# Moving w_in's shifted words and the values of single tiles to PSUM banks of their own, in a banded-attention and two-layer FFN kernel

## The chip, the cores and the metric

One core of a Trainium2 chip (trn2) runs the kernel. The metric is the device time of one execution in microseconds (us). A measured time is the median of several executions. The profiled execution is a further one, with the hardware profiler on.

## What is computed

Causal attention with a window of 64 positions over 8 batches, 8 heads, 576 positions and head dimension 64, in float32. Its output, as 4608 tokens of 512 features, goes through a two-layer network whose middle function is the identity for positive values and a factor alpha per feature for negative ones.

```python
scores = (1 / sqrt(D)) * q @ k.transpose(0, 1, 3, 2)
mask = (rel >= 0) & (rel < 64)
scores = where(mask, scores, -1e9)
attn = exp(scores - max(scores))
attn = attn / (sum(attn) + 1e-9)
x = (attn @ v).transpose(0, 2, 1, 3).reshape(4608, 512)
h = x @ w_in
g = maximum(h, 0) + alpha * minimum(h, 0)
out = g @ w_out
```

The weights w_in (512 x 2048) and w_out (2048 x 512) are passed to the kernel as 64-bit words and made into floats on the chip.

## The kernel before

**Tiles and blocks.** The 4608 tokens are 36 tiles of 128, and 4 tiles are a block, so there are 9 blocks of 512 tokens. For each tile the kernel computes scores (`score`, L448, on TensorE, into a pair of score banks `S_BANK[t % 2]`, banks 2 and 3 or 4 and 5), the masked row minimum of the negated scores for each of 8 heads (`take_least`, L457, VectorE), the exponentials and their sums (`exponential`, L464, ScalarE, 8 per tile), the reciprocal of the sums (`invert`, L468 and L469, VectorE), the scaled weights (`scale`, L473, GpSimd, called POOL in the profile), their transposes, the value matmuls (`value`, L504, TensorE) and x, split into a high part xh (L576 on ScalarE or L577 on VectorE) and a low part xl (L578, VectorE). The values lie in banks 6 and 7 (`V_BANK`).

**Single tiles.** The first eight tiles are attended one by one (`attend_one`), with due times from the list `SINGLE`. They are transposed on TensorE (`turn`, L488) back into their own score banks, and copied out of them (`take_turned`, L492). The values of a single tile lie in the first half (columns 0 to 255) of each of banks 6 and 7. Later tiles go in pairs (`attend_two`), whose values fill both halves; most of those are transposed on VectorE (L481, L483).

**First layer.** A cell is one block times one chunk of 128 of the 2048 middle features, in 12 matmuls of 128 x 512 (`cell`, L646: four of xh with the weight's high part wh, four of xl with wh, four of xh with the low part wl). The result in a bank (`H_BANK`, 0 or 1 in turn) is evicted by ScalarE (L652, the slope) and VectorE (L653, the maximum), and stored to memory by a DMA of SP's queue. A cell needs x of all four tiles of its block. For block 0, the first three chunks (`EARLY_HALVES`) are done as half cells of two tiles each, so that they can start when tiles 0 and 1 have x. Two half cells in a row share a bank and a buffer, one in each half. Due times come from `HALVES`, `PACE` and, for later blocks, `BEGIN` and `CELL`.

**Conversion of w_in.** Meanwhile `convert_in` makes the 16 chunks of w_in from 64-bit words (`chunk`). SP loads a chunk into one of three raw buffers (L343). ScalarE converts the low words (L352, ulps). VectorE scales the high words into PSUM (L357, "rebias"), shifts them there (L368) and joins them with the sign (L370) into `val`; POOL adds the ulps (L372). ScalarE or POOL makes wh (L325) and POOL or VectorE wl (L322). The shifted words, `aside`, lie in the second half (columns 256 to 511) of banks 6 and 7, in one two-bank tile `twin`; every chunk uses the same place.

**Second layer.** After all first-layer cells, `second` multiplies with w_out in a form with seven products in place of eight (L750).

**The order.** Every step is an `Op` with engine, assumed duration, keys that it reads and writes, and a due time (`add`). `Program.order` plays these on a model of the five engines, and gives each engine its instructions in the order of due time among those that are ready in the model. Then they are emitted in that order, and the framework inserts the semaphore waits that the tiles' accesses call for. The keys are what the planner knows of conflicts: `bank.6.0` and `bank.6.1` are two halves of bank 6, which it takes as independent. A step marked `paired` is modelled as sharing a port with POOL. From the end of `ident` until the half cell `h.0.1.0` is placed, the planner fills TensorE's gaps with matmuls of the identity (`warm`, L307). The four small operations `signs` (L312 to L315, VectorE) derive the slope from alpha.

Of the kernel before, what the change touches and what calls it, by code (L numbers as in the profile page):

```python
# [9 lines left out]
F32 = mybir.dt.float32  # L10
# [183 lines left out]
def banded_attention_then_prelu_ffn(  # L194
# [67 lines left out]
    staged = [stage[:, i] for i in range(2)]  # L262
    raws.append(stage.rearrange("p x t -> p (x t)").bitcast(I32))

    banks = [psum.tile([P, 512], F32, name=f"bank_{i}") for i in range(6)]
    twin = psum.tile([P, 1024], F32, name="bank_6")
    banks += [twin[:, :512], twin[:, 512:]]
    aside = twin.rearrange("p (x t) -> p x t", x=2)[:, :, 256:]
    H_BANK, S_BANK, V_BANK = (0, 1), ((2, 3), (4, 5)), (6, 7)

    hidden = [[far.tile([P, 4, 2, HW], F32, name=f"g_{n}_{d}") for d in range(DUOS)] for n in range(NB)]
# [7 lines left out]
    def add(name, engine, busy, emit, *args, **kw):  # L279
        p.add(name, {engine: (busy, emit)}, *args, **kw)  # L280
# [33 lines left out]
        nc.vector.tensor_tensor(out=slope, in0=sign, in1=alpha_p, op=ALU.mult)  # L314
        nc.vector.tensor_scalar(out=flip, in0=sign.bitcast(I32), scalar1=-2**31, scalar2=None, op0=ALU.bitwise_and)  # L315

    add("signs", "DVE", 0.5, signs, ["alpha"], ["signs"])


    def subtract_of(out, a, b):  # L320
# [14 lines left out]
    def chunk(name, c, f, second, start=0.0):  # L335
        r = raw_at[0] % (2 if second else RAWS)
        ulps, k_ulps = ulp_ring[raw_at[0] % 2], f"e.ulps.{raw_at[0] % 2}"
        raw_at[0] += 1
        raw = raws[r]
        if second:  # L340
            load = lambda: nc.sync.dma_start(raw, w_out[f * P:(f + 1) * P, :])
        else:
            load = lambda: nc.sync.dma_start(raw.rearrange("p (c f) -> p c f", c=NP),  # L343
                                             w_in[:, 2 * f * P:2 * (f + 1) * P].rearrange("(c p) f -> p c f", p=P))
        pairs = raw.rearrange("p (n t) -> p n t", t=2)
        low, high = pairs[:, :, 0].bitcast(U32), pairs[:, :, 1]
        at = val[:, c]
        bits = at.bitcast(I32)
        k_raw, k_val = ["e.staged.0", "e.staged.1"] if r == 2 else [f"e.raw.{r}"], f"e.val.{c}"
        both = keys(k_val + "a", k_val + "b")  # L350
        add("raw." + name, "SP", 0.5, load, (), keys(*k_raw), service=1.7, earliest=start)
        add("rd." + name, "ACT", 0.57, lambda: nc.scalar.activation(ulps, low, AF.Copy, scale=2.0**-29), k_raw, keys(k_ulps), earliest=start)  # L352
        two_of = lambda v: v.rearrange("p (x t) -> p x t", x=2)
        k_aside = [f"bank.{b}.1" for b in V_BANK]
        by_vector = not second and f in REBIASED
        if by_vector:
            add("rb." + name, "DVE", 0.64, lambda: nc.vector.tensor_scalar(  # L357
                out=aside, in0=two_of(high).bitcast(F32), scalar1=2.0**-112, scalar2=None, op0=ALU.mult), k_raw, k_aside, earliest=start)
        else:
            add("rb." + name, "ACT", 0.57, lambda: nc.scalar.activation(at, high.bitcast(F32), AF.Copy, scale=2.0**-112), k_raw, [*keys(k_val), *both], earliest=start)  # L360
        if second:
            add("sh." + name, "DVE", 0.52, lambda: nc.vector.tensor_scalar(
                out=bits, in0=bits, scalar1=3, scalar2=flip[:, f:f + 1], op0=ALU.logical_shift_left, op1=ALU.bitwise_or), ["signs"], [k_val], earliest=start, paired=True)
            add("sg." + name, "DVE", 0.62, lambda: nc.vector.scalar_tensor_tensor(  # L364
                out=bits, in0=high, scalar=-2**31, in1=bits, op0=ALU.bitwise_and, op1=ALU.bitwise_xor), k_raw, [k_val], earliest=start, paired=True)
        else:
            from_ = aside.bitcast(I32) if by_vector else two_of(bits)
            add("sh." + name, "DVE", 0.62, lambda: nc.vector.tensor_scalar(  # L368
                out=aside.bitcast(I32), in0=from_, scalar1=3, scalar2=None, op0=ALU.logical_shift_left), [] if by_vector else [k_val], k_aside, earliest=start)
            add("sg." + name, "DVE", 0.64, lambda: nc.vector.scalar_tensor_tensor(  # L370
                out=two_of(bits), in0=two_of(high), scalar=-2**31, in1=aside.bitcast(I32), op0=ALU.bitwise_and, op1=ALU.bitwise_xor), [*k_raw, *k_aside], [*keys(k_val), *both], earliest=start)
# [120 lines left out]
        copy(turned[t % 2][:, u].rearrange("p h u b q -> p b h u q"),  # L492
             banks[from_[u]].rearrange("p (b h u q) -> p b h u q", b=2, h=2, u=2))

    def value(t, i):
        av = [bank_of(b).rearrange("p (i a) q -> p i a q", i=2)[:, i] for b in V_BANK]
        pt, at = turned[t % 2].rearrange("p a h u b q -> p a h (u b q)"), 2 * (t % KRING)
        for a in range(2):
            for block, to, from_ in ((1, slice(0, P), slice(W, 3 * W)), (0, slice(0, W), slice(0, W)),
                                     (2, slice(W, P), slice(3 * W, 4 * W))):  # L500
                for h in range(2):
                    for x in range(2):
                        r, hs = slice(x * W, (x + 1) * W), slice(h * D, (h + 1) * D)
                        nc.tensor.matmul(av[x][hs, a, to], vring[r, a, at + block, hs], pt[r, a, h, from_],  # L504
                                         start=block == 1, stop=block == 2)
# [56 lines left out]
    def x_keys(part, slot, tiles=range(BT)):  # L562
        return [f"{part}.{slot}.{i}" for i in tiles]

    def x_parts(ts):
        n, i = divmod(ts[0], BT)
        here = slice(i * P, (i + len(ts)) * P)
        if len(ts) == 1:
            pieces = [(range(2), [part.rearrange("p (a x) t -> p x a t", x=2)[:, :, :, here] for part in xs[n % 2]],
                       twin.rearrange("p (x i a q) -> p x i a q", x=2, i=2, a=2)[:, :, 0], [f"bank.{b}.0" for b in V_BANK])]  # L570
        else:
            pieces = [([x], [part.rearrange("p (a x) (i q) -> p x i a q", x=2, q=P)[:, x, i:i + 2] for part in xs[n % 2]],
                       bank_of(V_BANK[x]).rearrange("p (i a) q -> p i a q", i=2), halves_of(V_BANK[x])) for x in range(2)]
# [7 lines left out]
    def attend_one(t, begin, pace):  # L581
# [4 lines left out]
                [key for a in pairs for key in (f"e.q.{t % 2}.{a}", *ring_keys("k", t, [a]))], [f"bank.{b}.{a}" for b in S_BANK[t % 2] for a in pairs], key=begin)  # L586
        softmax(t, True)
        turned_by_pe(t, S_BANK[t % 2], begin + 0.5 * pace)
        add(f"av.{t}", "PE", 1.0, lambda: value(t, 0), [*ring_keys("v", t), *pt_keys(t)], [f"bank.{b}.0" for b in V_BANK], key=begin + pace)
        x_parts([t])  # L590

    def values_of(ts, key):
        def emit():
# [34 lines left out]

    def cell(n, f, key, m=None):

        at = counted[0] + (counted[0] % 2 if m is None else 0)
        counted[0] = at + (2 if m is None else 1)
        bank, c = H_BANK[at // 2 % 2], at // 2 % len(cells)
        d, j, x = f % 8 // 2, f % 2, f // 8
        parts = [0, 1] if m is None else [at % 2]
        half = slice(0, 2 * HW) if m is None else slice(m * HW, (m + 1) * HW)
        to = slice(parts[0] * HW, (parts[-1] + 1) * HW)
        h, g = banks[bank][:, to], cells[c][:, to]
        k_h, k_g = [f"bank.{bank}.{i}" for i in parts], [f"cell.{c}.{i}" for i in parts]
# [222 lines left out]
```

## Time and profile before

| | |
|---|---|
| median of 3 runs | 851.5 us (850.8 to 851.97) |
| profiled execution | 852.4 us, span 850.6 us |
| busy: TensorE, VectorE, ScalarE, POOL | 838.3, 694.0, 438.3, 201.3 us |
| HBM read, written | 95.95 MB, 55.57 MB |

The profile's page gives busy times by engine; a line number there is that of the kernel file. "Idle before" a group of instructions names what the engine waited for last. PE is TensorE's matmul stream, DVE VectorE, ACT ScalarE. A busy time of PE is modelled, and matmuls overlap each other slightly.

### The profile page before, as it was taken

To read this page: it belongs to the slowest core of one execution; us is meant where nothing else is said; L and a number is where in the kernel's file an instruction comes from. 1 tells how busy PE (TensorE), PEld (TensorE's weight loads), DVE (VectorE), ACT (ScalarE), POOL (GpSimd) and SP (SyncE) were. 2 spreads that over 40 slices of the span, in tenths; PEclk is the share of its full clock that TensorE was granted. 3 is DMA by queue.
4 is the path that set the end of the run, shared out by engine and by line. 5 is a ranking of instruction groups with operands and counts; after the bars stand their busy time and mean duration, and the time that the engine had idled before them with its cause. 6 is when DMAs were issued, how large, how long until landed. Compare 5 with 4: busy or idle time off the path is not lost.

```text
span 850.6 us, 21098 instructions
## 1 busy us (share of the span) xinstructions
PE 838.3 (99%) x7850; PEld 758.5 (89%) x7850; DVE 694.0 (82%) x1777; ACT 438.3 (52%) x1111; POOL 201.3 (24%) x189
## 2 busy tenths in 40 slices
PE   8899999999999999999999999999999999999998
PEld 8778888888888888888888889999999999999998
DVE  5778898998989979898894647979798888879883
ACT  5777755556655565556643434444444444444441
POOL 5777414355611065212640000000000000000000
PEclk9999999999999999999999999999999999999999
DMA  8778655555655567656555997545354444545201
GB/s 253 232 238 253 212 164 195 161 163 201 212 162 174 185 227 247 200 177 220 190 203 183 319 307 256 164 111 169 110 156 137 139 135 137 150 126 164 84 27 50
DMA packets 121287, 152.91 MB, mean 180 GB/s; under 512 B 10592, under 2 KB 92512, under 8 KB 121184
## 3 DMA queue, kind: packets, MB, share of 16 engines
q1 hardware_dynamic: 120896, 151.30, 56.0%
q8 instruction: 62, 1.02, 0.5%
q14 instruction: 41, 0.34, 0.1%
q10 hardware_dynamic: 288, 0.26, 0.1%
HBM read 95.95 MB, written 55.57 MB: 178 GB/s over the span
## 4 chain that ended last, share of the span: by engine, by line
PE 90%; DVE 5%; DMA 2%; ACT 2%; issue 1%; SPq 0%; POOL 0%; DVEq 0%; POOLq 0%; ACTq 0%
PE bank L750 41%; PE bank L646 40%; PE bank L504 4%; PE bank L448 4%; DVE pt L481 1%; PE bank L488 1%; DVE cell L653 1%; ACT w L464 1%; DMA g<-g 1%; PE bank L307 1%; DMA v<-vN 1%; DVE pt L483 1%; DVE w L457 0%; DMA g<-cell 0%; DVE bank L368 0%
## 5 line engine op out<-in xcount | busy, mean ns | idle before, releaser
L722 ACT CAST yh<-g 128x512 fp32r<-128x512 f32 x216 | 133.0, 622 | 142.1 <-PE bank L750 85.9
L652 ACT ACTIVATE cell<-bank,alphas 128x512 f32<-128x512 f32 (+1 forms) x147 | 99.6, 678 | 160.1 <-PE bank L646 154.7
L723 DVE TENSOR_TENSOR yl<-g,yh 128x512 fp32r<-128x512 f32 x216 | 147.6, 687 | 26.1 <-ACT yh L722 25.0
L646 PE MATMUL bank<-xh,wh 128*128 128x512 f32 (+1 forms) x588 | 158.7, 392 | 0.5 <-DVE cell L653 0.2
L750 PE MATMUL bank<-wh,yh 128*128 128x256 f32 x1008 | 155.9, 277 | 0.0
L750 PE MATMUL bank<-wh,yl 128*128 128x256 f32 x1008 | 155.8, 277 | 0.0
L750 PE MATMUL bank<-wl,yh 128*128 128x256 f32 x1008 | 155.8, 277 | 0.0
L646 PE MATMUL bank<-xl,wh 128*128 128x512 f32 (+1 forms) x588 | 155.0, 385 | 0.0
L646 PE MATMUL bank<-xh,wl 128*128 128x512 f32 (+1 forms) x588 | 154.7, 385 | 0.0
L653 DVE SCALAR_TENSOR_TENSOR cell<-bank,alphas,cell 128x512 f32<-128x512 f32 (+1 forms) x147 | 108.0, 737 | 47.2 <-ACT cell L652 41.3
L750 PEld LDWEIGHTS bank<-wh,yh 128*128 128x128 f32 x1008 | 133.5, 188 | 0.2
L750 PEld LDWEIGHTS bank<-wh,yl 128*128 128x128 f32 x1008 | 133.5, 188 | 0.0
L750 PEld LDWEIGHTS bank<-wl,yh 128*128 128x128 f32 x1008 | 133.4, 188 | 0.0
L646 PEld LDWEIGHTS bank<-xl,wh 128*128 128x128 f32 x588 | 109.2, 188 | 22.6
L646 PEld LDWEIGHTS bank<-xh,wh 128*128 128x128 f32 x588 | 106.6, 188 | 25.2 <-DVE cell L653 2.9
L646 PEld LDWEIGHTS bank<-xh,wl 128*128 128x128 f32 x588 | 109.2, 188 | 22.2
L464 ACT ACTIVATE w<-w,nm 128x128 f32<-128x128 f32 x288 | 111.6, 390 | 25.0 <-DVE nm L457 25.0
L473 POOL TENSOR_TENSOR w<-w,rc 128x512 f32<-128x512 f32 x72 | 74.3, 1052 | 117.0 <-DVE rc L469 90.5
L481 DVE STREAM_TRANSPOSE pt<-w 32x256 f32<-32x256 f32 x192 | 83.7, 436 | 10.0 <-POOL w L473 6.7
L717 DVE TENSOR_TENSOR g<-g,g 128x512 f32<-128x512 f32 x108 | 74.2, 687 | 1.8
L457 DVE CUSTOM_DVE_ANT_0 w<-bank,masks 128x128 f32<-128x128 f32 x288 | 63.0, 285 | 7.4 <-PE bank L448 7.2
L372 POOL TENSOR_TENSOR val<-val,ulps 128x512 int32<-128x512 int32 x32 | 41.5, 1301 | 102.6 <-DVE val L364 91.2
(62 smaller groups left out, 717.7 us busy)
## 6 DMA issues: line engine op xcount, KB each, us to landing
g<-g SPq DMA_DIRECT2D x144, 256.0 KB, 3.4
g<-cell SPq DMA_DIRECT2D x141, 256.0 KB, 3.0
out<-cell SPq DMA_DIRECT2D x36, 256.0 KB, 2.5
q<-qT SPq DMA_DIRECT2D x35, 256.0 KB, 5.2
raw<-w_out SPq DMA_DIRECT2D x16, 512.0 KB, 5.1
v<-vN SPq DMA_DIRECT2D x18, 384.0 KB, 5.3
k<-kT SPq DMA_DIRECT2D x17, 384.0 KB, 4.6
raw<-w_in SPq DMA_DIRECT2D x11, 512.0 KB, 4.4
```

Of the source, the lines that this page charges most:

```text
L372: add("jn." + name, "POOL", 1.27, lambda: nc.gpsimd.tensor_tensor(out=bits, in0=bits, in1=ulps, op=ALU.add), [k_ulps], [k_val, *both], ear ...
L457: nc.vector.tensor_tensor_reduce(out=of_head(weights[t % 2], g), in0=bank_of(S_BANK[t % 2][x])[:, e].rearrange("p (b k) -> p b k", b=2), i ...
L464: nc.scalar.activation(w, w, AF.Exp, scale=-1.0, bias=least[t % 2][:, g:g + 1], accum_out=sums[:, t % 2, g, 0:1])
L473: nc.gpsimd.tensor_tensor(out=w, in0=w, in1=rc.unsqueeze(1).unsqueeze(3).broadcast_to(list(w.shape)), op=ALU.mult)
L481: nc.vector.transpose(to, w[:, x, j])
L646: nc.tensor.matmul(h, w[KEPT + f][:, a * P:(a + 1) * P], v[:, a, half], start=k == a == 0, stop=k == 2 and a == NP - 1, skip_group_check=True)
L652: add(f"sl.{name}", "ACT", 0.13 + 0.46 * part, lambda: nc.scalar.activation(g, h, AF.Copy, scale=slope[:, f:f + 1]), ["signs", *k_h], k_g)
L653: add(f"la.{name}", "DVE", 0.12 + 0.61 * part, lambda: nc.vector.scalar_tensor_tensor(out=g, in0=h, scalar=sign[:, f:f + 1], in1=g, op0=AL ...
L717: add(name, "DVE", 0.61, lambda: nc.vector.tensor_tensor(out=to(), in0=a(), in1=b(), op=op), reads, writes)
L722: add(f"ys.{u}.{i}.h", "ACT", 0.54, lambda: nc.scalar.copy(y_of(y_hi, x, hi), value()), [*ks, "late"], his)
L723: add(f"ys.{u}.{i}.l", "DVE", 0.61, lambda: nc.vector.tensor_tensor(out=y_of(y_lo, x, lo), in0=value(), in1=y_of(y_hi, x, hi).bitcast(F32) ...
L750: nc.tensor.matmul(banks[bank][:, h * EH:(h + 1) * EH], part[:, j * HW + h * P:j * HW + (h + 1) * P], w[k][:, j * EH:(j + 1) * EH], start= ...
```

## The change

`banks`: 6 and 7 are tiles of their own; 2 and 3, and 4 and 5, become two-bank tiles (`twins`). The shifted words of chunk c take the whole of bank 6 or 7 in turn (`V_BANK[c % 2]`). The values of single tile t lie in the first halves of its two score banks; the key of these steps is the whole of both banks. Each half cell takes a bank and a buffer of its own, so the count of cells goes up by one for half cells and whole cells alike. `signs` is marked as paired. The numbers BEGIN, SINGLE, HALVES, PACE and FIRST_TURN change.

```diff
-BEGIN = 10.0
+BEGIN = 11.0
-SINGLE = (3.0, 7.0, 11.0, 18.0, 24.0, 29.0, 35.0, 42.0)
-HALVES = (15.0, 21.0)
+SINGLE = (3.0, 3.0, 11.0, 15.0, 21.0, 32.0, 35.0, 41.0)
+HALVES = (14.0, 19.0)
-PACE = 3.4
-FIRST_TURN = 61.5
+PACE = 3.6
+FIRST_TURN = 60.0
...
-    banks = [psum.tile([P, 512], F32, name=f"bank_{i}") for i in range(6)]
-    twin = psum.tile([P, 1024], F32, name="bank_6")
-    banks += [twin[:, :512], twin[:, 512:]]
-    aside = twin.rearrange("p (x t) -> p x t", x=2)[:, :, 256:]
+    banks = [psum.tile([P, 512], F32, name=f"bank_{i}") for i in range(2)]
+    twins = [psum.tile([P, 1024], F32, name=f"bank_{2 + 2 * i}") for i in range(2)]
+    banks += [twin[:, x * 512:(x + 1) * 512] for twin in twins for x in range(2)]
+    banks += [psum.tile([P, 512], F32, name=f"bank_{i}") for i in (6, 7)]
...
-    add("signs", "DVE", 0.5, signs, ["alpha"], ["signs"])
+    add("signs", "DVE", 0.5, signs, ["alpha"], ["signs"], paired=True)
...
-        k_aside = [f"bank.{b}.1" for b in V_BANK]
+        aside, k_aside = banks[V_BANK[c % 2]], halves_of(V_BANK[c % 2])
...
-                out=aside, in0=two_of(high).bitcast(F32), scalar1=2.0**-112, ...
+                out=aside, in0=high.bitcast(F32), scalar1=2.0**-112, ...
...
-    def value(t, i):
-        av = [bank_of(b).rearrange("p (i a) q -> p i a q", i=2)[:, i] for b in V_BANK]
+    def value(t, i, by=V_BANK):
+        av = [bank_of(b).rearrange("p (i a) q -> p i a q", i=2)[:, i] for b in by]
...
-    def x_parts(ts):
+    def x_parts(ts, by=V_BANK):
...
-                       twin.rearrange(...)[:, :, 0], [f"bank.{b}.0" for b in V_BANK])]
+                       twins[ts[0] % 2].rearrange(...)[:, :, 0], halves_of(*by))]
...
-        add(f"av.{t}", "PE", 1.0, lambda: value(t, 0), [...], [f"bank.{b}.0" for b in V_BANK], key=begin + pace)
-        x_parts([t])
+        add(f"av.{t}", "PE", 1.0, lambda: value(t, 0, S_BANK[t % 2]), [...], halves_of(*S_BANK[t % 2]), key=begin + pace)
+        x_parts([t], S_BANK[t % 2])
...
-        at = counted[0] + (counted[0] % 2 if m is None else 0)
-        counted[0] = at + (2 if m is None else 1)
-        bank, c = H_BANK[at // 2 % 2], at // 2 % len(cells)
+        at = counted[0]
+        counted[0] += 1
+        bank, c = H_BANK[at % 2], at % len(cells)
...
-        parts = [0, 1] if m is None else [at % 2]
...
-        to = slice(parts[0] * HW, (parts[-1] + 1) * HW)
+        to = slice(0, half.stop - half.start)
...
-        k_h, k_g = [f"bank.{bank}.{i}" for i in parts], [f"cell.{c}.{i}" for i in parts]
+        k_h, k_g = halves_of(bank), [f"cell.{c}.{i}" for i in range(2)]
```

## Rows read from the trace of the kernel before

**Rows 1.** Stretches (us): busy (instructions) of PE, PEld, DVE, ACT, POOL, then clock, DMA

```profile
22.50:40.40 17.90, 13.93 (x249) 12.38 (x245) 13.62 (x52) 13.52 (x47) 14.71 (x13) 0.90 0.73 230
...
53.90:92.00 38.10, 38.10 (x421) 31.00 (x417) 29.93 (x76) 26.42 (x67) 28.11 (x25) 1.00 0.79 237
92.00:440.00 348.00, 347.73 (x3399) 291.06 (x3400) 313.12 (x1053) 198.73 (x626) 134.82 (x121) 1.00 0.59 192
```

**Rows 2.** The same view of line L307 alone (PE and PEld)

```profile
0.00:22.50 22.50, 13.25 (x86) 12.04 (x86) 1.00 0.85 254
```

**Rows 3.** Timeline of PE: start us, duration us, instruction [idle before, releaser]

```profile
18.87 1.13 PE L504 MATMUL bank<-pt,v 64*64 64x128 f32 x48 [0.71 <-ACT wh L325]
...
22.50 0.74 PE L646 MATMUL bank<-xh,wh 128*128 128x256 f32 x4
...
35.91 1.64 PE L504 MATMUL bank<-pt,v 64*64 64x128 f32 x48 [1.92 <-ACT pt L492]
37.26 3.18 PE L448 MATMUL bank<-k,q 64*64 64x128 f32 x64
40.37 0.74 PE L646 MATMUL bank<-xh,wh 128*128 128x256 f32 x4
...
52.82 1.13 PE L504 MATMUL bank<-pt,v 64*64 64x128 f32 x48 [1.25 <-DVE bank L368]
...
90.00 1.98 PE L448 MATMUL bank<-k,q 64*64 64x128 f32 x64
```

**Rows 4.** Timeline of DVE

```profile
15.41 0.69 DVE L357 TENSOR_SCALAR bank<-raw 128x512 f32<-128x512 f32 x1 [0.58 <-PE bank L504]
16.75 0.70 DVE L368 TENSOR_SCALAR bank<-bank 128x512 int32<-128x512 int32 x1 [0.66 <-ACT xh L576]
...
19.10 1.12 DVE L314 TENSOR_TENSOR alphas<-alphas 128x16 f32<-128x16 f32 x1
...
22.35 0.69 DVE L578 TENSOR_TENSOR xl<-bank,xh 128x512 fp32r<-128x512 f32 x1 [0.71 <-ACT xh L576]
...
39.80 0.69 DVE L578 TENSOR_TENSOR xl<-bank,xh 128x512 fp32r<-128x512 f32 x1 [0.70 <-ACT xh L576]
```

**Rows 5.** Timeline of ACT

```profile
16.62 1.27 ACT L492 COPY pt<-bank 128x512 f32<-128x512 f32 x2
...
21.73 0.58 ACT L576 CAST xh<-bank 128x512 fp32r<-128x512 f32 x1 [2.76 <-DVE bank L368]
...
31.55 0.83 ACT L652 ACTIVATE cell<-bank,alphas 128x256 f32<-128x256 f32 x2
...
33.73 0.58 ACT L576 CAST xh<-bank 128x512 fp32r<-128x512 f32 x1 [0.78 <-DVE val L370]
...
39.18 0.58 ACT L576 CAST xh<-bank 128x512 fp32r<-128x512 f32 x1 [1.93 <-DVE val L370]
```

**Rows 6.** Waits, 0 to 90 us: total us, times, longest us

```profile
DVE bank L357 <- PE bank L504: 4.2, 3, 1.8
```

**Rows 7.** One stretch of 1 us, columns as in rows 1

```profile
37.00:38.00 1.00, 1.00 (x36) 1.00 (x32) 0.40 (x1) 0.26 (x1) 1.00 (x2) 0.50 0.91 293
```

**Rows 8.** Timelines of POOL, PE and DVE, 83 to 95 us

```profile
83.39 2.54 POOL L322 TENSOR_TENSOR wl<-val,wh 128x512 fp32r<-128x512 f32 x2
...
86.28 1.07 PE L646 MATMUL bank<-xh,wl 128*128 128x512 f32 x4
...
94.81 1.07 PE L646 MATMUL bank<-xh,wh 128*128 128x512 f32 x4
...
86.56 0.69 DVE L578 TENSOR_TENSOR xl<-bank,xh 128x512 fp32r<-128x512 f32 x1
```

**Rows 9.** Timelines of ACT, DVE and PE, 46 to 62 us

```profile
46.86 1.05 ACT L492 COPY pt<-bank 128x512 f32<-128x512 f32 x2
...
55.41 0.69 DVE L578 TENSOR_TENSOR xl<-bank,xh 128x512 fp32r<-128x512 f32 x1 [0.26 <-ACT xh L576]
...
61.41 1.06 PE L448 MATMUL bank<-k,q 64*64 64x128 f32 x32
```

More of the change, by code (lines that the diff above doesn't have):

```diff
@@ L352, in chunk @@
         add("rd." + name, "ACT", 0.57, lambda: nc.scalar.activation(ulps, low, AF.Copy, scale=2.0**-29), k_raw, keys(k_ulps), earliest=start)
-        two_of = lambda v: v.rearrange("p (x t) -> p x t", x=2)
-        k_aside = [f"bank.{b}.1" for b in V_BANK]
+        aside, k_aside = banks[V_BANK[c % 2]], halves_of(V_BANK[c % 2])
         by_vector = not second and f in REBIASED
@@ L357, in chunk @@
             add("rb." + name, "DVE", 0.64, lambda: nc.vector.tensor_scalar(
-                out=aside, in0=two_of(high).bitcast(F32), scalar1=2.0**-112, scalar2=None, op0=ALU.mult), k_raw, k_aside, earliest=start)
+                out=aside, in0=high.bitcast(F32), scalar1=2.0**-112, scalar2=None, op0=ALU.mult), k_raw, k_aside, earliest=start)
         else:
@@ L366, in chunk @@
         else:
-            from_ = aside.bitcast(I32) if by_vector else two_of(bits)
+            from_ = aside.bitcast(I32) if by_vector else bits
             add("sh." + name, "DVE", 0.62, lambda: nc.vector.tensor_scalar(
@@ L370, in chunk @@
             add("sg." + name, "DVE", 0.64, lambda: nc.vector.scalar_tensor_tensor(
-                out=two_of(bits), in0=two_of(high), scalar=-2**31, in1=aside.bitcast(I32), op0=ALU.bitwise_and, op1=ALU.bitwise_xor), [*k_raw, *k_aside], [*keys(k_val), *both], earliest=start)
+                out=bits, in0=high, scalar=-2**31, in1=aside.bitcast(I32), op0=ALU.bitwise_and, op1=ALU.bitwise_xor), [*k_raw, *k_aside], [*keys(k_val), *both], earliest=start)
         add("jn." + name, "POOL", 1.27, lambda: nc.gpsimd.tensor_tensor(out=bits, in0=bits, in1=ulps, op=ALU.add),
@@ L569, in x_parts @@
             pieces = [(range(2), [part.rearrange("p (a x) t -> p x a t", x=2)[:, :, :, here] for part in xs[n % 2]],
-                       twin.rearrange("p (x i a q) -> p x i a q", x=2, i=2, a=2)[:, :, 0], [f"bank.{b}.0" for b in V_BANK])]
+                       twins[ts[0] % 2].rearrange("p (x i a q) -> p x i a q", x=2, i=2, a=2)[:, :, 0], halves_of(*by))]
         else:
@@ L588, in attend_one @@
         turned_by_pe(t, S_BANK[t % 2], begin + 0.5 * pace)
-        add(f"av.{t}", "PE", 1.0, lambda: value(t, 0), [*ring_keys("v", t), *pt_keys(t)], [f"bank.{b}.0" for b in V_BANK], key=begin + pace)
-        x_parts([t])
+        add(f"av.{t}", "PE", 1.0, lambda: value(t, 0, S_BANK[t % 2]), [*ring_keys("v", t), *pt_keys(t)], halves_of(*S_BANK[t % 2]), key=begin + pace)
+        x_parts([t], S_BANK[t % 2])
     def values_of(ts, key):
```

## The prediction

> **What bounds the kernel now.** Read the span by stretches first [rows 1]. From 53.9 us to 92 us TensorE is busy for all of its 38.10 us, and from 92 to 440 us it idles 348.00 - 347.73 = 0.27 us. So what lies behind 53.9 us is a solid block of matmuls, and the end moves only if that block starts earlier or if a hole is torn into it. What can be won lies ahead: 17.90 - 13.93 = 4.0 us idle between 22.5 and 40.4, one idle stretch of 1.25 us at 52.82 [rows 3], and, before 22.5 us, filler (matmuls of the identity, L307), 13.25 us of it [rows 2].
>
> Two gates set the start. The first half cell runs at 22.50 [rows 3]; it needs x of tiles 0 and 1. After the three early halves the next cell runs at 40.37 [rows 3]; it needs x of tiles 2 and 3, whose last parts are xh of tile 3 at 39.18 [rows 5] and its xl at 39.80 [rows 4].
>
> Now see what these chains wait for. VectorE's rebias of a w_in chunk (L357) idles 0.58 us for the value matmuls (L504), its shift (L368) 0.66 us for xh, then xl 0.71 us for xh [rows 4]. In turn xh of tile 1 starts at 21.73 after 2.76 us idle put down to the shift L368, and xh of tiles 2 and 3 idle 0.78 and 1.93 us for L370 [rows 5]. No data passes between L504 or xh and these three lines: values lie in columns 0 to 255 of banks 6 and 7, shifted words in columns 256 to 511. The trace orders them by bank all the same. Over the first 90 us L357 alone waits 4.2 us for L504, in 3 places [rows 6]. The planner's keys name the halves apart, so it wrote an order in which such waits hold up in-order engines.
>
> **The change, part by part.** I leave each engine's order as it is and take out the waits that go; the order that the planner writes anew makes the bounds.
>
> *Gate 1.* From 15.4 to 22.4 us VectorE has 0.58 + 0.66 + 0.71 = 1.95 us idle on shared banks [rows 4]. What follows it (row minima of tile 2, then the exponentials of tiles 2 and 3 back to back on ScalarE) comes that much earlier: **-1.95 us**. Least: 0, if another wait fills it. Most: value of tile 1 needs only the turned copies, which end at 16.62 + 1.27 = 17.89 [rows 5], and runs at 18.87 for 1.13 us [rows 3]; its xh could start near 19.1 in place of 21.73, hence -2.6 us.
>
> *Gate 2.* xh of tile 2 loses its 0.78 us; the turned copies of tile 3, next on ScalarE, and the value of tile 3 at 35.91 follow: **-0.8 us** (0 to -1.9, TensorE's idle ahead of that value). The value ends at 35.91 + 1.64 = 37.55, but L368 and L370 slip in ahead of xh at 39.18, put there by the bank: **-1.6 us** (0 to -1.6). The value also ran at the lower clock: the granted clock is 0.50 of full at 37 to 38 us [rows 7], the 1.2 GHz level, after the 1.92 us of idle; value 1.64 us against 1.13, scores 3.18 against 1.98 [rows 3]. With TensorE waiting less I take **-0.5 us**, the value's part (0 to -1.7, both).
>
> *Later.* The value of tile 4, at 52.82, waits 1.25 us for L368 [rows 3]: **-1.25 us** (0 to -1.25). Behind 53.9 us TensorE never waits, so what VectorE gains there changes nothing now.
>
> *What is added.* (a) Scores of tile t+2 now wait until xl of tile t has left the score banks. Scores of tiles 4 and 5 ran together at 37.26, inside the wait for xl of tile 3; tile 5's half, about 1 us at full clock (half of 1.98), falls behind that gate: **+1.0 us** (0 to 1.6, half of 3.18). (b) Half cells own a bank, so the third waits for the eviction of the first, which ScalarE began at 31.55 with two in 0.83 us [rows 5], behind all exponentials. Either one eviction is put amid the exponentials, 0.83/2 = 0.4 us on the chain, or the half cell's three groups of matmuls, at most 0.74 us each as at 22.50 [rows 3], move behind gate 2: **+0.5 us** (0.4 to 2.2), near the first, since an eviction that a matmul waits for gets an early due time. (c) Shifted words take one whole bank, as many elements as before; L357 takes 0.69 us and L368 0.70 [rows 4]. That one bank is dearer or cheaper than two halves no row shows: 0, and by that spread of 0.01 us over 48 operations 0.5 either way, on an engine with holes. (d) The score banks become two-bank tiles. Were these ordered as one, a tile's second transposes would wait for the first copy, 1.27/2 = 0.6 us, for tiles 1 and 3 on the chain; I take 0, because the transposes of one bank and the copy of the other have separate keys and separate banks (0 to 1.2). (e) Signs are marked as sharing a port with POOL: the third of its operations took 1.12 us [rows 4] on 16 columns. The mark changes only the plan: 0, bounds -1.0 to +1.0, that operation gone or met once more. (f) BEGIN, SINGLE, HALVES, PACE and FIRST_TURN alter due times and the earliest times of loads, so SP's and POOL's queues get another order too. Behind 53.9 us TensorE's backlog covers that; without it each late load would be paid. 0, bounds -0.3 (all idle there) to +1.2 (one more wait like that at 52.82).
>
> Sum: -1.95 - 0.8 - 1.6 - 0.5 - 1.25 + 1.0 + 0.5 = **-4.6 us**. The profiled execution took 852.4 us (span 850.6), 0.9 above the median of 851.5; so 847.8 on its terms and **846.9** against the median. Ceiling: all idle (4.0 + 1.25), the lost clock (1.7) and 2.6 us of filler gone make -9.5, so 842.0.
>
> **Rivals.**
>
> *The clock falls sooner* (chance 0.14). Filler stops once the second half cell is placed. That comes earlier, so a thinly filled stretch follows earlier. For it: the fall to 0.50 after 1.92 us of idle [rows 3, 7]. Against: over 22.5 to 40.4 us the clock still averaged 0.90 [rows 1]. Price: the value of tile 2 at 1.64 in place of 1.13 us (0.5), the scores of tile 3 at 3.18/2 in place of 1.98/2 (0.6), and the clock's 0.5 of the sum not won: 846.9 + 1.6 = 848.5. "TensorE: The Clock Gate" of the Trainium skill, section "HAM oscillation — how this bites in real kernels", speaks against gaps between short runs of matmuls in this way; the fall at 37 us agrees.
>
> *The weights do not follow* (0.13). POOL makes the low halves of chunks 13 and 14 in 2.54 us from 83.39 on, the first done near 84.66; cell 13 first reads it at 86.28 [rows 8]: 1.6 us of slack. If the conversion keeps its times, TensorE waits there and keeps 1.6 us of its gain: 849.9, within 0.2%. Against it: from 53.9 to 92 us VectorE is busy 29.93 of 38.10 us and POOL 28.11 [rows 1], and VectorE loses bank waits there as well.
>
> *Score banks held too long* (0.11), the slower side. Tile 7's xl runs at 86.56, the next block's first cell at 94.81 [rows 8], or near 90 after the gain. Before, score banks were free after the turned copies; now after xl, for tile 4 (55.41 + 0.69) - (46.86 + 1.05) = 8.2 us later [rows 9]. If two generations (4 and 5, then 6 and 7) paid that in full, 16.4 us less the 4.85 by which gate 2 comes earlier, tile 7 would end 11.5 us later, at 98.8, and TensorE would stand 4 us past its old time: 855.5. It decides once that xl passes 90. Against: scores of tile 6 ran at 61.41, already 5.3 us behind xl of tile 4 [rows 9].
>
> *The change doesn't remove the waits*: before tile 8 no other owner is left in banks 6 and 7, so this has little room; it stays in the forecast's spread.
>
> **How the numbers follow.** Forecast 0.62, its own range 843 to 849; clock 0.14; weights 0.13; score banks 0.11. About 0.2% (1.7 us) is what a measurement of this kernel can tell from no change. Faster: 0.62 + 0.14 = 0.76; same 0.13; slower 0.11. The range reaches from about the ceiling, 841.5, to just past no change, 851.8; outside are the slower rival and thin ends of the others, 0.2 in all.
>
> **What would show it.** Right: no wait of L357, L368 or L370 on L504, nor of xh on those, ahead of 60 us; first half cell at 19 to 20.6 us; xl of the fourth tile at 34 to 37; less than 12 us of filler; solid TensorE from about 50. Wrong: granted clock 0.50 for over 4 us between 20 and 40; TensorE waiting for weights at cells 10 to 15, or for xl of tiles 4 to 7; over 1 us idle behind 60 us.

## The result, and the profile after

| | before | after |
|---|---|---|
| median | 851.61 us (850.8 to 852.74, 6 runs) | 859.83 us (858.0 to 862.07, 6 runs) |
| profiled execution | 852.4 us, span 850.6 us | 860.36 us, span 858.6 us |
| TensorE busy | 838.3 us | 847.6 us |

The changed kernel is slower: the ratio is 1.0095, with the interval 1.0079 to 1.0112. The forecast of 846.9 us was wrong, and 859.83 us lies outside its range, 841.5 to 851.8.

**Where the time comes from.** Cut the span at the second layer. These are the first and last rows of its matmuls in TensorE's timeline; each row merges four. The kernel before:

```profile
502.05 0.63 PE L750 MATMUL bank<-wh,yh 128*128 128x256 f32 x4
...
846.11 0.64 PE L750 MATMUL bank<-wh,yl 128*128 128x256 f32 x4
```

The kernel after:

```profile
499.53 0.63 PE L748 MATMUL bank<-wh,yh 128*128 128x256 f32 x4
...
853.43 0.63 PE L748 MATMUL bank<-wh,yl 128*128 128x256 f32 x4
```

The second layer starts 502.05 - 499.53 = 2.5 us earlier, so the part of the kernel that the prediction worked on did gain. (Profiled executions with the same early part scatter by about 1 us here: 502.05 to 503.12 in the kernel before, e2, e3 and e5, 499.53 to 500.22 in the kernel after, e1 and e4.) But from first to last row it takes 853.43 - 499.53 = 353.9 us in place of 344.1: 9.8 us lost, in a stage that the prediction never looked at. Behind the last row the span goes on for 5.2 us in place of 4.5. Together: -2.5 + 9.8 + 0.7 = 8.0 us, the difference of the spans.

The page's groups say the same of the second layer. Before, then after (mean ns of one, then idle time before the group):

```profile
L750 PE MATMUL bank<-wh,yh 128*128 128x256 f32 x1008 | 155.9, 277 | 0.0
```

```profile
L748 PE MATMUL bank<-wh,yh 128*128 128x256 f32 x1008 | 159.0, 280 | 0.8 <-DVE cell L756 0.8
```

There is one wait, of 0.8 us, put down to VectorE's eviction L756, and each of the three groups of 1008 (one is shown) has become about 3.1 us longer. The wait in TensorE's timeline after:

```profile
583.41 0.62 PE L748 MATMUL bank<-wl,yh 128*128 128x256 f32 x4
583.87 0.62 PE L748 MATMUL bank<-wh,yl 128*128 128x256 f32 x4
585.29 0.71 PE L748 MATMUL bank<-wh,yh 128*128 128x256 f32 x4 [0.81 <-DVE cell L756]
585.84 0.63 PE L748 MATMUL bank<-wl,yh 128*128 128x256 f32 x4
586.31 0.63 PE L748 MATMUL bank<-wh,yl 128*128 128x256 f32 x4
```

Compare starts. Ahead of the wait four matmuls follow in 583.87 - 583.41 = 0.46 us, behind it in 586.31 - 585.84 = 0.47. That looks like nothing, but it stays so to the end. Counts of matmuls in the same 50 us show it (stretch, busy and count of TensorE, clock, DMA). Before, then after:

```profile
520.00:570.00 50.00, 50.00 (x444) 1.00 0.50 149
600.00:650.00 50.00, 50.00 (x444) 1.00 0.44 132
```

```profile
520.00:570.00 50.00, 50.00 (x443) 1.00 0.48 137
600.00:650.00 50.00, 50.00 (x427) 1.00 0.43 127
```

Both kernels run at one pace between 520 and 570 us, 50/444 = 112.6 ns for a matmul. After the wait the changed kernel needs 50/427 = 117.1 ns, with the granted clock at 1.00, TensorE without idle time and no more DMA than before. So the wait cost 585.29 - 583.87 - 0.46 = 0.96 us itself, and the 2280 matmuls behind it (3024 less 62 pieces of 12 ahead of it, counted below) cost 117.1 - 112.6 = 4.5 ns more each, 10.3 us. That is 11.2 us together, some 1.4 more than the 9.8 by which the layers differ: the layer of before pays a smaller wait of the same kind, below, which e2 measures at 1.3 us.

**Who waits for whom.** VectorE's timeline after:

```profile
577.25 0.68 DVE L756 TENSOR_TENSOR cell<-bank,r 128x512 f32<-128x512 f32 x1
...
584.47 0.68 DVE L756 TENSOR_TENSOR cell<-bank,r 128x512 f32<-128x512 f32 x1
```

The second layer uses all eight banks as accumulators in a ring, seven products to a block of 512 tokens, so product `at` of block `n` lies in bank (7n + at) mod 8. A block goes through its seven products in four rounds, and what one round adds to a product is a piece of 12 matmuls; pieces are counted through from 0. The matmul that waits, in piece 2 * 28 + 6 = 62, opens the last product of block 2 (blocks count from 0): bank (14 + 6) mod 8 = 4. Bank 4 last held the sixth product of block 1, whose eviction `d12` is the one at 577.25, long done. The one at 584.47 is `d21`, the last eviction of block 1: it reads bank (7 + 6) mod 8 = 5, and ends at 584.47 + 0.68 = 585.15, just ahead of 585.29. Banks 4 and 5 are one two-bank tile after the change, and the waits fit a framework that orders accesses to it as one. (The row of the weight loads puts the same stop, 0.98 us there, down to a cast of ScalarE, L720. e1 below, which changes nothing but the tiles, has neither wait, so it is the tile.) The planner's keys know the banks apart, so it gave `d21` a late place and saw no wait. By the same sum the two-bank tile of before, banks 6 and 7, meets this only in block 8, (56 + 6) mod 8 = 6. Its gap is there in TensorE's timeline before, at 815.42 (0.56 us from start to start in place of 0.45), 0.15 us behind the end of VectorE's eviction L758 (814.59 + 0.68 = 815.27), with few matmuls left to lose on:

```profile
814.86 0.62 PE L750 MATMUL bank<-wh,yl 128*128 128x256 f32 x4
815.42 0.71 PE L750 MATMUL bank<-wh,yh 128*128 128x256 f32 x4
```

**The early part.** Stretches after, as in [rows 1], then the filler's alone, as in [rows 2]:

```profile
22.50:40.40 17.90, 14.73 (x229) 12.92 (x221) 12.97 (x52) 13.52 (x46) 12.57 (x13) 0.81 0.71 221
...
53.90:92.00 38.10, 38.10 (x416) 30.79 (x415) 31.36 (x105) 27.57 (x77) 29.99 (x27) 1.00 0.81 253
92.00:440.00 348.00, 348.00 (x3408) 292.83 (x3407) 312.85 (x1026) 197.55 (x617) 134.21 (x119) 1.00 0.59 192
```

```profile
0.00:22.50 22.50, 13.09 (x86) 11.97 (x86) 1.00 0.86 256
```

TensorE is solid behind 40.4 us now. The granted clock of the gap's stretch fell from 0.90 to 0.81, and the filler is what it was. TensorE's timeline after, with the rows that answer to [rows 3]:

```profile
17.18 0.63 PE L487 MATMUL bank<-ident,w 128*128 128x128 f32 x4 [0.60 <-ACT pt L491]
...
21.67 1.10 PE L447 MATMUL bank<-k,q 64*64 64x128 f32 x32
22.71 0.74 PE L644 MATMUL bank<-xh,wh 128*128 128x256 f32 x4
...
28.78 0.66 PE L487 MATMUL bank<-ident,w 128*128 128x128 f32 x4 [1.73 <-POOL w L472]
30.21 0.94 PE L487 MATMUL bank<-ident,w 128*128 128x128 f32 x4 [0.77 <-ACT pt L491]
31.82 1.99 PE L503 MATMUL bank<-pt,v 64*64 64x128 f32 x48 [0.67 <-ACT pt L491]
...
35.35 1.20 PE L644 MATMUL bank<-xh,wh 128*128 128x256 f32 x4
...
37.77 1.13 PE L503 MATMUL bank<-pt,v 64*64 64x128 f32 x48
...
39.71 0.74 PE L644 MATMUL bank<-xh,wh 128*128 128x256 f32 x4
```

And the granted clock of the stretch in which the value of tile 2 took 1.99 us:

```profile
31.00:37.00 6.00, 5.33 (x65) 5.07 (x65) 3.99 (x7) 3.74 (x8) 4.06 (x4) 0.50 0.73 219
```

The first half cell runs at 22.71 (before 22.50), gate 2 opens at 39.71 (40.37). A tile's second transposes wait for the first copy, 0.60 us in tile 1 (17.18) and 0.77 us in tile 2 (30.21). The third half cell went from 26.8 to 35.35, in front of the value of tile 3, which went from 35.91 to 37.77. The clock was at its 1.2 GHz level, 0.50, through these 6 us; before, through the 2 us from 37 to 39. Of the 2.5 us that the second layer starts earlier, gate 2 gives 0.7 and the wait gone at 52.82 us 1.25; the rest is idle time that the kernel before had later on, 0.27 us between 92 and 440 us and 55.00 - 54.76 = 0.24 between 440 and 495, and the kernel after has not.

### The profile page after: what moved, and what is told of

It reads as the page before. It is cut to its first block, busy times and chain, and to the rows that moved or that the text cites. A ratio compares the mean times of both kernels' runs of the same rounds, so it can differ in the third digit from the quotient of the medians.

```text
span 858.6 us, 21067 instructions
## 1 busy us (share of the span) xinstructions
PE 847.6 (99%) x7850; PEld 769.2 (90%) x7850; DVE 696.8 (81%) x1777; ACT 438.2 (51%) x1110; POOL 201.9 (24%) x190
## 4 chain that ended last, share of the span: by engine, by line
PE 97%; ACT 1%; DVE 1%; issue 0%; POOL 0%; DVEq 0%; POOLq 0%
PE bank L644 46%; PE bank L748 41%; PE bank L503 4%; PE bank L447 4%; PE bank L487 1%; ACT w L463 1%; PE bank L307 1%; ACT pt L491 0%; DVE cell L756 0%; DVE xl L577 0%; DVE alphas L312 0%; ACT ulps L352 0%; DVE val L369 0%; POOL w L472 0%; DVE w L456 0%
## 5 line engine op out<-in xcount | busy, mean ns | idle before, releaser
L720 ACT CAST yh<-g 128x512 fp32r<-128x512 f32 x216 | 132.7, 621 | 146.2 <-PE bank L748 94.7
L748 PE MATMUL bank<-wh,yh 128*128 128x256 f32 x1008 | 159.0, 280 | 0.8 <-DVE cell L756 0.8
L748 PE MATMUL bank<-wh,yl 128*128 128x256 f32 x1008 | 158.9, 280 | 0.0
L748 PE MATMUL bank<-wl,yh 128*128 128x256 f32 x1008 | 158.9, 280 | 0.0
L748 PEld LDWEIGHTS bank<-wh,yh 128*128 128x128 f32 x1008 | 136.5, 189 | 1.1 <-ACT yh L720 1.0
L748 PEld LDWEIGHTS bank<-wh,yl 128*128 128x128 f32 x1008 | 135.7, 189 | 0.0
L748 PEld LDWEIGHTS bank<-wl,yh 128*128 128x128 f32 x1008 | 135.6, 189 | 0.0
L482 DVE STREAM_TRANSPOSE pt<-w 32x128 f32<-32x128 f32 x192 | 58.1, 303 | 3.9
```

What stands on the lines that cost most here:

```text
L482: nc.vector.transpose(to[:, :, j ^ 1], w[:, x, j, :, j ^ 1])
L720: add(f"ys.{u}.{i}.h", "ACT", 0.54, lambda: nc.scalar.copy(y_of(y_hi, x, hi), value()), [*ks, "late"], his)
L748: nc.tensor.matmul(banks[bank][:, h * EH:(h + 1) * EH], part[:, j * HW + h * P:j * HW + (h + 1) * P], w[k][:, j * EH:(j + 1) * EH], start= ...
```

## The experiments

The theory: what is lost is lost in the second layer, by two-bank tiles that are ordered as one, and by a pace that a wait of TensorE breaks. The rivals: the pace comes from something else that the change brought (a later VectorE, other DMA), or the early part is the cause.

**e1_after_apart: the banks as single tiles once attention is over.** All eight banks keep their numbers; the two-bank tiles are given back after the first layer.

```diff
-    twins = [psum.tile([P, 1024], F32, name=f"bank_{2 + 2 * i}") for i in range(2)]
+    doubles = early.enter_context(tc.tile_pool(name="doubles", bufs=1, space=PSUM))
+    twins = [doubles.tile([P, 1024], F32, name=f"bank_{2 + 2 * i}") for i in range(2)]
...
+        apart = ctx.enter_context(tc.tile_pool(name="apart", bufs=1, space=PSUM))
+        for i in range(2, 6):
+            banks[i] = apart.tile([P, 512], F32, name=f"bank_{i}_late")
```

> Theory A (the two-bank tile is guarded as one, and the wait that this puts on TensorE at 584 us ends a faster pace of the second layer's matmuls): banks 2 to 5 are separate tiles again from the second layer on, so no wait of TensorE near 584 us, one matmul per 113 ns from about 511 us to the end, second layer 343 us in place of 354, time 848.3 us (859.8 - 11.5), between 847 and 850. Theory B (the pace goes with the place of the banks or with the new order of the first layer, not with the wait): 858 to 860, matmuls at 118 ns from about 584 us as before.

Measured: 848.89 us (847.35 to 849.89), ratio to before 0.9961 (0.9949 to 0.9973), the fastest of all kernels here, ahead of both the kernel before and the one after. The second layer has no wait of TensorE and keeps its pace, in the counts of its stretch:

```profile
600.00:650.00 50.00, 50.00 (x444) 1.00 0.46 136
```

So the whole loss of 8.2 us hung on how banks 2 to 5 are declared in the second layer, and without it the change gains 3.0 us.

**e2_before_apart: the same for banks 6 and 7 of the kernel before.** The diff is that of e1, for `twin` and for the banks 6 and 7.

> The kernel before, with banks 6 and 7 as separate tiles from the second layer on. Theory A: its only wait of TensorE in the second layer, at 815 us, is gone and the pace stays at 113 ns, so 0.2 + 0.2 us of gaps and some 275 matmuls x 4.4 ns = 1.2 us less: 850.0 us (from 851.6). Theory B: 851.6, the slower pace still begins near 814 us.

Measured: 851.02 us (850.45 to 852.14), ratio 0.9992 (0.9983 to 1.0001): hardly to be told from no change. The gap at 815 is gone, and from first to last row the second layer takes 845.85 - 503.12 = 342.7 us in place of 344.1. The stretch from 820 to 840 us, behind the place of the gap, holds 179 matmuls in place of 173, at a clock of 1.00 in both. The theory's sign holds and the pace is kept; the size in the time is at the edge of what can be measured.

**e3_before_ring: the kernel before, with its two-bank tile met in block 2.** Only the numbers of the ring change, so that bank 6 comes where 4 was.

```diff
-            acc[i] = bank_ring[0] % 8
+            acc[i] = (0, 1, 2, 3, 6, 7, 4, 5)[bank_ring[0] % 8]
```

> The kernel before with one change: in the second layer the banks are taken in the order 0 1 2 3 6 7 4 5, so that the one two-bank tile (6, 7) stands where banks 4 and 5 stood. Theory A: the wait moves from 815 us to about 587 us (0.3 to 0.8 us long), and 228 us of matmuls go at 118 in place of 113 ns: 2010 x 4.4 ns = 8.9 us more, 860.9 us in all, between 859 and 862. Theory B: the time of before, 851.6, within 0.5.

Measured: 852.5 us in the median, ratio 1.0052 (1.0012 to 1.0092). The ten executions form two groups with nothing between: four at 861.78 to 862.79, six at 851.03 to 852.54. The profiled one is of the upper group; its timeline and its stretch:

```profile
586.78 0.62 PE L750 MATMUL bank<-wh,yl 128*128 128x256 f32 x4
587.33 0.71 PE L750 MATMUL bank<-wh,yh 128*128 128x256 f32 x4
587.87 0.64 PE L750 MATMUL bank<-wl,yh 128*128 128x256 f32 x4
588.35 0.63 PE L750 MATMUL bank<-wh,yl 128*128 128x256 f32 x4
```

```profile
600.00:650.00 50.00, 50.00 (x427) 1.00 0.42 127
```

A wait of about 0.1 us (0.55 from start to start in place of 0.45) where the sum of the ring puts it, and from there 427 matmuls in 50 us. The matmul starts 0.15 us behind the end of the eviction L758 (586.50 + 0.68 = 587.18). Nothing else of the change is in this kernel, so the rivals fall: a wait of a tenth of a microsecond can cost 10 us. But the 860.9 us expected came in four executions of ten only. The two groups lie some 10 us apart, as much as 2280 matmuls at 4.5 ns, so the other six may have had no such wait, or have had it and kept the pace; which was not seen, since only one was profiled.

**e5_before_no_steps: the kernel before without its stepped addresses.** The list `SHIFTS` says at which column each piece finds its operands; in pieces 4 to 7 of the second layer they step by 16 columns, elsewhere they stand still.

```diff
-    SHIFTS = [(1, 1)] * 4 + [(i, i) for i in range(4)] + [(1, 1)] * 280
+    SHIFTS = [(1, 1)] * 288
```

> The kernel before, with the stepped addresses of the second layer's products 4 to 7 left out (all buffers read 16 columns in). If the steps set the pace: 118 ns per matmul from the first to the last, so 2665 matmuls x 4.4 ns = 11.7 us more, 863.3 us. If the pace comes by itself after some 11 us: 851.6.

Measured: 864.69 us (863.7 to 864.7, 4 runs), ratio 1.0142 (1.0125 to 1.0159). The view of the second layer's line gives shortest, median and longest duration of a matmul. The kernels before, after, and this one:

```profile
L750 PE MATMUL bank<-wh,yh x1008: 276/276/356, 502.1 to 845.5; 128*128 128x256 f32 x168
```

```profile
L748 PE MATMUL bank<-wh,yh x1008: 276/281/355, 499.5 to 852.8; 128*128 128x256 f32 x168
```

```profile
L750 PE MATMUL bank<-wh,yh x1008: 280/281/281, 502.8 to 857.9; 128*128 128x256 f32 x168
```

Before has its median at 276 ns, after has some at 276 and its median at 281, and without the steps none of this line is ever at 276. So the fast pace did not come by itself: four pieces with stepped addresses set it, and it then held until a wait of TensorE broke it. TensorE's timeline after shows it set in, 96 matmuls behind the start of the layer, right behind pieces 4 to 7; from 510.41 to the next start are 0.47 us, from 510.88 on 0.45:

```profile
510.41 0.63 PE L748 MATMUL bank<-wh,yl 128*128 128x256 f32 x4
510.88 0.62 PE L748 MATMUL bank<-wh,yh 128*128 128x256 f32 x4
511.33 0.62 PE L748 MATMUL bank<-wl,yh 128*128 128x256 f32 x4
```

**e4_after_walk: the kernel after, with the steps once more behind the wait** (pieces 64 to 67).

```diff
-    SHIFTS = [(1, 1)] * 4 + [(i, i) for i in range(4)] + [(1, 1)] * 280
+    SHIFTS = [(1, 1)] * 4 + [(i, i) for i in range(4)] + [(1, 1)] * 56 + [(i, i) for i in range(4)] + [(1, 1)] * 280
```

> The changed kernel with the four stepped addresses that the second layer's products 4 to 7 use (buffers read 0, 16, 32 and 48 columns in) used a second time in products 64 to 67, right behind the wait. Theory A1 (the steps set the pace, a wait loses it): 113 ns again from about 591 us on, so 2200 x 4.4 ns = 9.7 us less than 859.8: 850.1. Theory A2 (a wait ends the pace for good): 859.8. Theory B: 859.8.

Measured: 853.27 us in the median, 848.22 to 859.47, ratio 1.0018 (0.9989 to 1.0046). The steps mend it in part: 850.1 us was expected, and of ten executions five lie at 848.2 to 851.8, four near 855, one at 859.5. In the profiled one (851.41) the wait of 0.81 us is there as in the kernel after, and the fast pace is back from 594.46 on. It also shows the second meeting, block 4 with (28 + 6) mod 8 = 2:

```profile
585.86 0.71 PE L748 MATMUL bank<-wh,yh 128*128 128x256 f32 x4 [0.81 <-DVE cell L756]
...
594.46 0.62 PE L748 MATMUL bank<-wh,yh 128*128 128x256 f32 x4
...
662.00 0.62 PE L748 MATMUL bank<-wh,yl 128*128 128x256 f32 x4
662.55 0.71 PE L748 MATMUL bank<-wh,yh 128*128 128x256 f32 x4
663.10 0.62 PE L748 MATMUL bank<-wl,yh 128*128 128x256 f32 x4
...
843.98 0.62 PE L748 MATMUL bank<-wl,yh 128*128 128x256 f32 x4
844.44 0.62 PE L748 MATMUL bank<-wh,yl 128*128 128x256 f32 x4
```

Here a gap as long as that of e3 did not break the pace (0.46 us for four to the end). So a wait can break it and need not. What decides stays open. A pace lost at 662 us for good would add some 7.2 us (1608 matmuls at 4.5 ns), so 855 to 859 from where the five lie; the others may be such, but none of them was profiled.

**What the early part is worth.** The rest is measured on e1, where the second layer is quiet.

**e9_apart_old_numbers** is e1 with BEGIN, SINGLE, HALVES, PACE and FIRST_TURN as they were; **e10_before_new_numbers** is e2 with the new five.

```diff
-BEGIN = 11.0
-SINGLE = (3.0, 3.0, 11.0, 15.0, 21.0, 32.0, 35.0, 41.0)
-HALVES = (14.0, 19.0)
+BEGIN = 10.0
+SINGLE = (3.0, 7.0, 11.0, 18.0, 24.0, 29.0, 35.0, 42.0)
+HALVES = (15.0, 21.0)
...
-PACE = 3.6
-FIRST_TURN = 60.0
+PACE = 3.4
+FIRST_TURN = 61.5
```

> e1_after_apart with the five numbers of the kernel before (BEGIN, SINGLE, HALVES, PACE, FIRST_TURN): the structure alone. If the gain of the first layer comes from the banks, and the numbers only follow: second layer starts at 500.2 +- 0.7 us, time 848.9 +- 0.7. If the banks need the new numbers (a tile's scores now wait for xl two tiles ahead): TensorE waits for xl L578 or for the copies ahead of 60 us, second layer starts after 501.5, time 850.3 or more.

> e2_before_apart with the five new numbers: the numbers alone. If they only follow the banks: 851.0 as e2_before_apart, or up to 2 us more, since the waits between L504 and L357, L368, L370 stay. If they are where the gain is: 849.5 or less.

Measured: 849.74 us (849.38 to 850.87), ratio 0.9982 (0.9973 to 0.9992), and 854.0 us (853.56 to 855.7), ratio 1.003 (1.002 to 1.0039). So most of the gain is the new banks' own; by the medians the new numbers are worth 849.74 - 848.89 = 0.9 us with them, which is little beside the spread of the runs, and cost 854.0 - 851.02 = 3.0 us without, more than the 2 us expected at most.

**e8_apart_shared_cells: e1 with the counting of before,** two half cells to a bank.

```diff
-        at = counted[0]
-        counted[0] += 1
-        bank, c = H_BANK[at % 2], at % len(cells)
+        at = counted[0] + (counted[0] % 2 if m is None else 0)
+        counted[0] = at + (2 if m is None else 1)
+        bank, c = H_BANK[at // 2 % 2], at // 2 % len(cells)
...
```

> As e1_after_apart, but the half cells share banks and buffers by twos as in the kernel before. Theory C (the third half cell, waiting for a bank until the first is evicted, falls behind the exponentials and holds up the value of tile 3; that is why the change stands 4.5 us behind at 32 us): the third half cell at about 27 us again, value of tile 3 about 1.5 us earlier, second layer starts 1 to 2 us earlier, 498.2 to 499.2, time 847.4. Rival (the half cell only fills idle time): 848.9, within 0.5.

Measured: 852.31 us (850.93 to 852.95), ratio 1.0002 (0.9993 to 1.0011), 3.4 us above e1. The third half cell is back at its early place, and the value of tile 3 too (35.81; in the kernel after 37.77), and gate 2 opens at 37.90 us in place of e1's 39.99. But behind it TensorE waits for VectorE, and the second layer starts at 503.65 us, where 498.2 to 499.2 was expected (e1: 500.22):

```profile
26.94 0.64 PE L646 MATMUL bank<-xh,wh 128*128 128x256 f32 x4
...
37.90 0.74 PE L646 MATMUL bank<-xh,wh 128*128 128x256 f32 x4 [1.01 <-ACT xh L576]
...
93.18 1.10 PE L448 MATMUL bank<-k,q 64*64 64x128 f32 x32 [1.31 <-DVE xl L578]
...
103.79 1.20 PE L646 MATMUL bank<-xh,wh 128*128 128x512 f32 x4 [1.10 <-DVE cell L653]
...
118.36 1.20 PE L646 MATMUL bank<-xh,wh 128*128 128x512 f32 x4 [0.76 <-DVE cell L653]
```

**e6_apart_two_pieces: no two-bank tile at any time.** Each of the banks 2 to 7 is a tile, and x of a single tile is made in two pieces, one for each bank.

```diff
-            pieces = [(range(2), [part.rearrange("p (a x) t -> p x a t", x=2)[:, :, :, here] for part in xs[n % 2]],
-                       twins[ts[0] % 2].rearrange("p (x i a q) -> p x i a q", x=2, i=2, a=2)[:, :, 0], halves_of(*by))]
+            pieces = [([x], [part.rearrange("p (a x) t -> p x a t", x=2)[:, x, :, here] for part in xs[n % 2]],
+                       bank_of(by[x]).rearrange("p (i a) q -> p i a q", i=2)[:, 0], halves_of(by[x])) for x in range(2)]
```

> The changed kernel without any two-bank tile: x of a single tile is copied in two pieces, one for each score bank. Theory D (a tile's second transposes wait for the first copy since both banks are one tile, 0.6 and 0.8 us at 16.6 and 29.4 us, on the chain of the first layer's start): no such wait; second layer's first matmul at 498.9 to 499.6 us in place of 500.2 with banks apart in the second layer alone; time 847.5 to 848.3. Rival (the shorter pieces cost as much on ScalarE and VectorE as the wait gave): 848.9, within 0.5. Second layer as in e1_after_apart: 343 us, no wait.

Measured: 851.68 us (850.73 to 852.58), ratio 0.9998 (0.9989 to 1.0007). The transposes no longer wait for the copies, but TensorE waits 1.9 us for VectorE's evictions, at 103 and 118 us again, and the second layer starts at 503.46 us in place of the 498.9 to 499.6 expected.

**e7_apart_filler: e1 with the filler kept up until the last early half cell.** It is written to a free part of its bank.

```diff
-        nc.tensor.matmul(banks[H_BANK[1]][:, :P], ident, ident, start=True, stop=True)
+        nc.tensor.matmul(banks[H_BANK[1]][:, 256:256 + P], ident, ident, start=True, stop=True)
...
-    order = p.order(("ident", "h.0.1.0"))
+    order = p.order(("ident", "h.0.2.0"))
```

> As e1_after_apart, with filler kept on until the third half cell is placed (in columns 256 to 383 of bank 1). Theory E (the clock falls at 30 us since TensorE is thinly filled from 27 to 32 us, and work of 3 us takes 6): granted clock 1.00 over 22 to 40 us, 2 to 3 us less for that work, of which about 2 us reach the end: second layer starts at 498.2, time 847.0. Rival (the filler's bank makes it wait for evictions, or what follows is held by VectorE): 848.9 or more.

Measured: 850.04 us (848.96 to 850.43), ratio 0.9977 (0.9967 to 0.9988). The clock never falls; the stretch that holds the 1.2 GHz level, in e1 and then here:

```profile
32.00:40.40 8.40, 8.40 (x151) 7.98 (x151) 4.48 (x8) 5.40 (x11) 5.81 (x5) 0.65 0.67 195
```

```profile
32.00:40.40 8.40, 8.19 (x168) 7.56 (x169) 5.61 (x19) 7.24 (x18) 7.45 (x7) 1.00 0.71 218
```

Gate 2 opens at 38.75 us in place of e1's 39.99, so the lower clock cost 1.2 us there. And yet the end is not earlier: the medians are 850.04 and 848.89 us, and e1's second layer starts at 500.22 us, this one's at 500.78. A part of what is lost on the way is idle time: between 92 and 440 us TensorE now idles 348.00 - 347.14 = 0.9 us and e1 did not. The profile names no releaser for it.

**e11_two_early** is e1 with two early half cells in place of three (`EARLY_HALVES = 2`); **e12_two_early_filler** adds e7's filler to it, which there ends with the first half cell of tiles 2 and 3.

```diff
-EARLY_HALVES = 3
+EARLY_HALVES = 2
```

> e1_after_apart with two early half cells in place of three, so that none waits for an eviction. Theory C (the third half cell, run at the lower clock in front of tile 3's value, holds it up by about 1 us): value of tile 3 at about 36.8 us in place of 37.8, second layer starts at 499.3 to 499.9, time 848.2. Rival (its work is only moved behind the gate and gives the same back): 848.9 to 849.5.

> e11_two_early with filler kept on until the first half cell of the second kind (in columns 256 to 383 of bank 1). Theory E (the clock): 1.00 over 22 to 40 us, value of tile 3 at about 35 us, second layer starts at 498 to 499, time 847.0. Rival (another wait behind takes it back, as in e7_apart_filler): 848.5 to 850.

Measured: 850.91 us (850.0 to 851.52), ratio 0.9987 (0.9978 to 0.9996), and 854.31 us (853.63 to 855.47), ratio 1.0033 (1.0022 to 1.0043). Both lie above what either side expected. In e11 the value of tile 3 comes at 36.20 us, but gate 2 opens at 39.83, hardly before e1's 39.99. With the filler the clock stays at 1.00, and TensorE idles 348.00 - 345.75 = 2.25 us between 92 and 440 us, where e11 idles nothing.

In e6, e7, e8 and e12 what was won at gate 2 was given back, and more, before the second layer; TensorE's waits behind 90 us are a part of that, and the rest was not traced. VectorE is busy 31 of 38 us from 53.9 to 92 in the kernel after (the stretches above), so a TensorE that comes earlier may meet its evictions late, and the planner writes another order each time. Which of these waits is due to the earlier TensorE and which to the new order was not separated.

## Why the prediction was wrong, by its steps

- **"The end moves only if that block starts earlier or if a hole is torn into it."** This is the step that failed. It looks at where that block starts and whether it has holes, and so reads busy time as work done. A hole was torn, of 0.96 us, but most of the loss came behind it: from 600 to 650 us TensorE was busy all the time in both kernels, and these 50 us held 444 matmuls in the one and 427 in the other. There is a third way for the end to move, the pace inside the block; the view that shows it is the count beside the busy time.
- **(d), the two-bank tiles.** The prediction asked the right question, whether they are ordered as one, and answered 0 with bounds 0 to 1.2, from the planner's keys. They are ordered as one. Its own [rows 6] could not tell: values and shifted words shared banks as well as a tile, and it read the waits as by bank. Early it made two transposes wait, 0.60 and 0.77 us, about what its upper bound of 1.2 us was made of; in the second layer, where the same banks are accumulators, it cost 9.8 us. The place was missed: every step that uses a bank whose declaration changes has to be listed, not only the steps that the diff edits. The row that could have shown it was in the trace of before, the gap at 815 us.
- **Gate 1, forecast -1.95 us: nothing.** The waits between different owners of a bank did go, though xl still waits 0.60 us for its own xh at 17.56. But in TensorE's order 14 matmuls of filler (19.92) and the scores of tile 2 stand ahead of the first half cell, the scores at 21.67 us now and at 21.47 before; that kept 22.71. The low part of tile 1 came earlier (21.04 against 22.35) and gained nothing by it. Why the planner kept the scores there stays open.
- **Gate 2, forecast -4.85 us in all: -0.7** (39.71 against 40.37). A part was never won at gate 1, and the next two points ate of the rest: e8, where the third half cell is early and the clock stays at 1.00, opens gate 2 at 37.90.
- **(a), +1.0 us, came as forecast**: only one tile's scores are left ahead of gate 2 (38.73), the next take 1.10 us at 44.23, behind it.
- **(b), the third half cell, forecast +0.5 us.** It took the other of the two ways named there: it moved behind the exponentials, to 35.35, in front of the value of tile 3. Its bound of 2.2 us holds the 37.77 - 35.91 = 1.9 us by which that value came later. Those are not the half cell's alone, since the clock was low as well; e11, without that half cell and with the clock still low, has the value at 36.20 and gains nothing at the gate.
- **"The clock falls sooner" came true**: 0.50 over 31 to 37 us, the value of tile 2 at 1.99 us. The Trainium skill's page "TensorE: Matmul & The Clock Gate", section "HAM oscillation — how this bites in real kernels", warns of gaps between short runs of matmuls; this fall, behind idle times of 1.73 and 0.77 us (28.78 and 30.21), agrees. Its price at gate 2 was 1.2 us, at the end nothing: e7, without it, ends no earlier than e1.
- **Later, -1.25 us, was right**: the value of tile 4 waits no more, and TensorE has no wait from 40.4 to 440 us.
- **"The weights do not follow" and "score banks held too long" did not occur** in the kernel after: no wait of TensorE on either from 40 to 440 us. The slower side came by a mechanism that no rival had.
- **(f), the numbers, costed at 0 within -0.3 to +1.2:** -0.9 us with the new banks and +3.0 without (e9, e10). They suit the structure of the change and not the one of before.
- **(c) and (e)** were not tested by a run of their own. An operation of `signs` still took long, 1.28 us at 19.36, and it is another than before [rows 4].

Of the signs that it named, the one of a clock at 0.50 for over 4 us came. Of those for being right TensorE's solid stretch came (from 40.4 us on); the first half cell at 19 to 20.6 us (22.71), xl of the fourth tile at 34 to 37 (39.59) and less than 12 us of filler (13.09) did not.

In sum: the forecast for the part ahead of the second layer was -4.6 us, and -2.5 came; the second layer was taken as untouched and lost 9.8. With it mended (e1) the change is worth 848.89 - 851.9 = -3.0 us against its own runs of before, so 848.9 us, at the upper edge of the forecast's own range of 843 to 849. That is partly luck: of the terms only (a) and the one at 52.82 us came as forecast, and 0.5 us of the gain is later idle time that it did not count.

## What to carry to other kernels

Compare counts in equal stretches as well as busy time: an engine that is busy all the time can lose 4% of its pace, as it did here from 600 to 650 us. Before buffers are joined into one tile, list everybody who uses any of them in any stage, since accesses to the tile may be ordered as one while a hand-made planner believes them apart; where the joined form is needed in one stage only, give it back after that stage. And tuned due times belong to one structure: change both together, and try the structure alone.

## What the runs showed of the hardware

A stream of matmuls of 128 x 256, each with its own weights, has two steady paces at the same granted clock of 1.00: 112.6 and 117.1 ns from start to start. Operands at stepped addresses in four pieces of 12 matmuls set the fast one (e5 and e4), and it held for hundreds of microseconds. A wait of TensorE of 0.1 to 1 us can end it for the rest of the kernel (the kernel before at 815 us, the kernel after, e3), or leave it (e4 at 662 us). What in the chip holds this state, and which waits break it, no run here tells.
